# A transformer block on one core: four row blocks of the third unit take their maxima over rectified differences, four later ones no longer do, GpSimd normalises rows in one instruction, and the order of the work is searched anew

## The chip, the cores and the metric

The kernel runs on one core of a Trainium2 chip. A core has TensorE (PE, matrix products into the eight banks of PSUM), VectorE (DVE), ScalarE (ACT), GpSimd (POOL, which works on SBUF alone) and SyncE (SP), which here issues every DMA. The metric is the device time of one execution in microseconds (us), as the median of several runs.

## The reference

A sequence of 2048 rows of 512 is normalised once. The result goes through an attention with 32 heads of 16 and, beside it, through a gated feed-forward layer of width 1792; both are added to the input.

```python
x = A_x                                   # [1, 2048, 512], bf16
xn = _layernorm(x, axis=-1)
# attention: H = 32, Dh = 16
scores = jnp.einsum("bhqd,bhkd->bhqk", q, k) * (Dh ** -0.5)
p = _softmax(scores, axis=-1)
o = jnp.einsum("bhqk,bhkd->bhqd", p, v)
# feed-forward
h = _silu(gate) * up
return x + _A_ref(xn, A_wqkv, A_wo) + _B_ref(xn, B_w1, B_w3, B_w2)
```

## The kernel before, in words

**Tiling.** Four heads make a head group, and 512 queries a query chunk: 8 x 4 pairs of them, the outer loop over chunks. A pair is cut into units of 256 queries (4 x 128 for the last four pairs, 128 + 128 + 256 for the first), 73 units in all. Units 0, 1 and 2 are the first pair.

**Two passes for each unit.** The first pass finds the maximum of each query's scores. TensorE multiplies 128 queries of one head with 512 keys into a PSUM bank (`p1_cand`, L1476), and VectorE reduces two banks at a time to two maxima (L1529, output `part`). One such bank is called a block here; a row block is the four blocks that belong to 128 queries of one head, two reductions. When a unit is complete, `final_max` combines the maxima: on GpSimd for most units (L1651 to L1665), by a small reduction on VectorE (L1688, `negm`) for units 0 and 1 and for those from 62 on. The negative maximum is written beside the queries as two more rows (`Z`, then `QT`), by a matrix product and a copy for units 0, 1 and the last nine (copy on ScalarE L1135, or on VectorE L1131 for the very last), through DMAs for the others. The second pass (`p2_cand`, L1796, or through a block-diagonal copy `BD` of the queries, L835) computes the scores again, keys by queries, now with the maximum subtracted, and ScalarE takes the exponentials into `PT`: one bank (L1821) or, where two lie ready, two banks in one instruction (L1852). `tile_PV` multiplies with the values, whose seventeenth column of ones gives the sums. The last four units are normalised on VectorE (transposes and reciprocal, L1901 to L1905), the others through GpSimd and DMAs.

**Split blocks.** For every second unit from 20 to 42, one row block goes another way: TensorE writes the difference of the scores of two key quarters into a bank (`d_cand`, L1585 and L1588, with the negated queries `QN` made by GpSimd in `split_prep`, L1552), ScalarE rectifies it (L1597, `RB`), and VectorE adds the second quarter and takes the maximum over both pairs in one instruction (L1522, a custom operation with an accumulator). It takes the place of two reductions, and costs ScalarE two Relus.

**The head.** Rows are loaded, their mean and variance taken by VectorE (L872, L875) or ScalarE (L862, L866), the factor by GpSimd (L886, L889). Groups of two row tiles are normalised by VectorE (L902) for the first three groups, and by GpSimd for the other five, as x * r + b: two small operations make b = −mean * r (L893, L895), one applies it (L912). TensorE transposes the result, and products with the weights follow. Keys and queries of the other head groups go through a scratch tensor in DRAM to be spread over partitions: `kq` by ScalarE (L1023), a DMA to `kd` or `qd` (L994), a DMA back into `KT` (L1011) or `QT` (L1016). `HEAD_K` is the position at which the first of these key tiles is due.

**What sets the order.** While the program is built, a planner keeps a time for each engine and picks, again and again, the candidate that can start first among those of the five engines (`pick_dve`, `pick_act`, `pick_pe`, `pick_pool`, `pick_sp`). Rules such as `A_LEAD` (how far ahead of VectorE the first pass is issued) or `PAIR_WAIT` (how long an exponential waits for a second one) may change every twelve positions: `TUNE` names for each stretch an entry of `SETS`. The planner's picks are the program's order on each engine, and each instruction waits on semaphores for what it needs.

## Time and profile before

| | |
|---|---|
| median of 3 runs | 1180.97 us (1180.08 to 1181.68) |
| span of the profiled execution | 1178.6 us (the page gives the span alone for this execution) |
| instructions | 35702 |
| GpSimd busy | 449.4 us (38%) |
| TensorE's granted clock | 1.00 in every stretch of 30 us up to 1170, 0.89 after it |
| chain that ended last | ACT 55%, DVE 31%, PE 11% |

The rest of the profile is shown with the prediction. In its rows, a timeline gives the start, the duration from the first start to the last end, engine, line, operation, output and input with sizes, and how many instructions are merged; in brackets stands the idle time ahead of it and what ended it. Instructions of one engine overlap a little, so the spacing of starts is what one more of them costs. Group rows give count, busy time and mean duration, then the idle time ahead. SPq is SyncE's queue of DMA issues.

### The profile page before, as it was taken

How to read it: one execution, taken by the hardware profiler on the slowest of the kernel's cores; microseconds unless marked ns; L12 is line 12 of the kernel's file. 1: busy time of each engine (PE TensorE's matmuls, PEld its weight loads, DVE VectorE, ACT ScalarE, POOL GpSimd, SP SyncE). 2: the span in 40 equal slices, each digit the busy share in tenths (PEclk: the TensorE clock that was granted, in tenths of full speed). 3: DMA queues.
4: the chain of work that ended last, by engine and by line, in shares of the span. 5: the costliest groups of instructions: out<-in, count | busy, mean ns of one | idle time of the engine just before them, and what ended most of it. 6: DMA issues, size and time to landing. Idle time of an engine off the chain costs nothing.

```text
span 1178.6 us, 35702 instructions
## 1 busy us (share of the span) xinstructions
PE 1111.9 (94%) x14770; PEld 512.0 (43%) x14922; DVE 1165.0 (99%) x1089; ACT 1158.5 (98%) x2130; POOL 449.4 (38%) x886
## 2 busy tenths in 40 slices
PE   8999999999999999999989999999999999899988
PEld 4444334434344433334434444434444443356654
DVE  8999999999999999999999999999999999999996
ACT  8899999999999999999999999999999999999998
POOL 7245534244424246244432222455632126432211
PEclk9999999999999999999999999999999999999999
DMA  8323232111121121111110111221210121001001
GB/s 250 82 70 80 61 91 58 48 29 40 31 49 32 31 67 35 46 39 30 45 27 24 30 43 28 60 52 44 54 30 22 43 57 36 25 22 29 11 11 28
DMA packets 140966, 55.79 MB, mean 47 GB/s; under 512 B 103296, under 2 KB 140804, under 8 KB 140804
## 3 DMA queue, kind: packets, MB, share of 16 engines
q1 hardware_dynamic: 140804, 53.50, 17.7%
q8 instruction: 118, 1.93, 0.7%
q14 instruction: 44, 0.36, 0.1%
HBM read 38.93 MB, written 6.74 MB: 39 GB/s over the span
## 4 chain that ended last, share of the span: by engine, by line
ACT 55%; DVE 31%; PE 11%; issue 1%; DMA 0%; POOL 0%; ACTq 0%; SPq 0%
ACT PT L1821 35%; DVE part L1529 31%; ACT PT L1852 13%; PE ps L835 4%; PE ps L839 3%; PE ps L1796 3%; PE ps L1476 2%; ACT zg L1191 1%; ACT ub L1195 1%; ACT th L1185 1%; ACT RB L1597 1%; ACT U L1919 1%; ACT kq L1023 0%; DMA PT<-in_A_x_dram 0%; ACT osb L1264 0%
## 5 line engine op out<-in xcount | busy, mean ns | idle before, releaser
L1529 DVE TENSOR_REDUCE part<-ps 128x2 f32<-128x1024 f32 x1000 | 1133.9, 1207 | 0.4 <-PE ps L1796 0.2
L1821 ACT ACTIVATE PT<-ps 128x512 bf16<-128x512 f32 x1498 | 799.6, 660 | 2.6 <-PE ps L1796 2.0
L1796 PE MATMUL ps<-QT,KT 32*128 32x256 bf16 (+1 forms) x3768 | 455.1, 258 | 9.0 <-ACT PT L1852 2.8
L1476 PE MATMUL ps<-KT,QT 32*128 32x512 bf16 x2048 | 417.1, 383 | 5.6 <-DVE part L1529 2.1
L1852 ACT ACTIVATE PT<-ps 128x1024 bf16<-128x1024 f32 x275 | 292.2, 1097 | 0.2
L1796 PEld LDWEIGHTS ps<-QT,KT 32*128 32x128 bf16 x3768 | 167.2, 92 | 164.0 <-issue 71.5
L839 PE MATMUL ps<-PT,Vaug 128*17 128x256 bf16 (+1 forms) x4672 | 185.5, 261 | 5.0 <-ACT PT L1852 2.7
L835 PE MATMUL ps<-xnT,ident 128*128 128x512 bf16 (+3 forms) x569 | 151.9, 324 | 24.5 <-ACT PT L1852 7.3
L1476 PEld LDWEIGHTS ps<-KT,QT 32*128 32x128 bf16 x2048 | 104.4, 91 | 141.8 <-issue 59.4
L835 PE MATMUL ps<-xnT,w 128*128 128x512 bf16 (+3 forms) x542 | 141.5, 330 | 8.3 <-ACT U L1919 2.3
L1944 POOL TENSOR_TENSOR Rc<-Lc,mone 128x8 f32<-128x8 f32 (+1 forms) x69 | 104.8, 1519 | 91.6 <-DMA Lc<-U 91.6
L839 PEld LDWEIGHTS ps<-PT,Vaug 128*17 128x17 bf16 x4672 | 88.0, 89 | 75.6 <-issue 51.1
L835 PE MATMUL ps<-BD,KT 128*128 128x256 bf16 (+1 forms) x604 | 103.6, 262 | 0.9 <-ACT PT L1852 0.3
L1658 POOL TENSOR_TENSOR mx<-part 128x16 f32<-128x16 f32 (+1 forms) x60 | 14.2, 236 | 233.9 <-DVE part L1529 233.7
L835 PEld LDWEIGHTS ps<-xnT,ident 128*128 128x128 bf16 x626 | 49.2, 97 | 105.2 <-ACT PT L1821 37.6
L835 PE MATMUL ps<-w,hT 128*128 128x128 bf16 (+3 forms) x326 | 77.9, 304 | 2.3 <-issue 1.0
L1162 POOL TENSOR_SCALAR t<-th 128x512 f32<-128x512 bf16 x56 | 34.7, 620 | 100.8 <-ACT th L1185 99.2
L835 PEld LDWEIGHTS ps<-xnT,w 128*128 128x128 bf16 x584 | 43.1, 97 | 67.4 <-issue 33.3
L1166 POOL TENSOR_TENSOR hT<-a,t 128x512 bf16<-128x512 f32 x56 | 71.0, 1268 | 2.5
L1164 POOL TENSOR_TENSOR a<-zg,ub 128x512 f32<-128x512 bf16 x56 | 64.5, 1153 | 7.5 <-ACT ub L1195 7.5
L835 PEld LDWEIGHTS ps<-BD,KT 128*128 128x128 bf16 x604 | 50.6, 98 | 22.5 <-ACT PT L1852 2.2
L1980 POOL TENSOR_TENSOR on_b<-U,R 128x256 bf16<-128x256 f32 (+1 forms) x33 | 23.4, 710 | 93.6 <-DMA R<-rd 93.5
(114 smaller groups left out, 722.8 us busy)
## 6 DMA issues: line engine op xcount, KB each, us to landing
w<-in_B_w_dram SPq DMA_DIRECT2D x112, 128.0 KB
R<-rd SPq DMA_DIRECT2D x55, 128.0 KB
QT<-qd SPq DMA_DIRECT2D x31, 128.0 KB
KT<-kd SPq DMA_DIRECT2D x28, 128.0 KB
BD<-QT SPq DMA_DIRECT2D x220, 10.5 KB
xr<-in_A_x_dram SPq DMA_DIRECT2D x16, 128.0 KB
out_dram<-osb SPq DMA_DIRECT2D x16, 128.0 KB
qd<-kq SPq DMA_DIRECT2D x15, 128.0 KB
```

Of the source, the lines that this page charges most:

```text
L835: return e.matmul(bank(bk)[:, c0 + a:c0 + b], make_lhsT(0, 128), rhs_ap(0)[:, a:b], start=start, stop=stop, **kw)
L839: ins = e.matmul(bank(bk)[32 * i:32 * i + m, c0 + a:c0 + b], make_lhsT(i), rhs if (a, b) == (0, ncols) else rhs[:, a:b], start=start, stop ...
L1162: q.append(_Item(lambda e: e.tensor_scalar(t1[:, :], th[:, ss, :], 1.0, 1.0, ALU.mult, ALU.add), [("th", ss)], [("t1",)], 0.62, 0.72))
L1164: q.append(_Item(lambda e: e.tensor_tensor(a32[:, :], zg[:, ss, :], ub[:, ss, :], ALU.mult), [("zg", ss), ("ub", ss)], [("a32",)], 1.1, 1.25))
L1166: q.append(_Item(lambda e: e.tensor_tensor(hT[:, hslot(idx), :], a32[:, :], t1[:, :], ALU.mult), [("a32",), ("t1",)], [("hT", hslot(idx))] ...
L1476: ins = e.matmul(bank(held[i]), QT[32 * j:32 * j + 32, qs, q * 128:(q + 1) * 128], KT[32 * j:32 * j + 32, g, c_ * 512:(c_ + 1) * 512], sta ...
L1529: redq.append(_Item(lambda e: e.tensor_reduce(dst, banks, AX.X, ALU.max), writes, [("part", par, i_) for i_ in ix[:m]], _c_dve(512 * m), c ...
L1796: ins = e.matmul(bank(b)[:, i * nq:(i + 1) * nq], KT[32 * j:32 * j + 32, g, (k0 + i) * 128:(k0 + i + 1) * 128], QT[32 * j:32 * j + 32, qs, ...
L1821: expq.append(_Item(lambda e: e.activation(PT[:, sl, :], bank(b), ACTF.Exp, scale=SCALE), [("ps", b)], [("PT", sl)], _c_act(512), cb=cb, e ...
L1852: return _Item(lambda e: e.activation(PT[:, s0:s1 + 1:s1 - s0, :], two_banks(b0, b1), ACTF.Exp, scale=SCALE), [("ps", b0), ("ps", b1)], [( ...
L1944: poolq["nrm"].append(_Item(lambda e: e.tensor_tensor(Rc[:, pp, 0:nl], Lc[:, pp, 0:nl], mone[:, 0:nl], ALU.pow), [("Lc", pp), ("mone",)], ...
L1980: poolq["nrm"].append(_Item(lambda e: e.tensor_tensor(onorm[ob][:, oslot(ob, g), q0:q0 + nq], U[:, us, 0:nq], R[:, pp, 0:nq], ALU.mult), [ ...
```

## The change

Unit 2's first 128 queries have four row blocks, one for each head; all four become split blocks, at the end of the unit's list. Three of them write their rectified differences not to `RB` but to slots 10 to 21 of `hT`, the buffer of the feed-forward layer's inner values, so each of the four has a buffer of its own (`HEAD_LOOK` is the number of positions by which their differences may run ahead). Units 36, 38, 40 and 42 lose their split block. GpSimd's normalisation becomes (x − mean) * r, with the mean as the scalar operand, and the two small operations are gone. `HEAD_K` goes from 14 to 8. The planner's cost of a split block's reduction is raised, and `SETS` and `TUNE` are other tables, with 219 entries instead of 189.

```diff
-    HEAD_K = 14
+    HEAD_K = 8
...
-    SPLITS = ((20, 44, 2), (58, 58, 2))
+    SPLITS = ((20, 36, 2), (58, 58, 2))
+    SPLIT_ROWS = 1
+    HEAD_SPLITS = {2: ((0, 0), (0, 1), (0, 2), (0, 3))}
+    HEAD_BUFS = (10, 14, 18)
+    HEAD_LOOK = 24
...
     SETS = (
         dict(),
-        dict(P2_FRAG=0.0, URG_WAIT=0.05, A_LEAD=0.82, PAIR_WAIT=0.15),
+        dict(FILL_SLIP=0.0, P1_SLIP=0.15),
...
-    SPLIT = {u: ((units[u][3] // 128 - 1, 3),) for lo, hi, st in SPLITS for u in range(lo, hi, st)}
+    SPLIT = {u: tuple((units[u][3] // 128 - 1, 3 - r) for r in range(SPLIT_ROWS)) for lo, hi, st in SPLITS for u in range(lo, hi, st)}
+    SPLIT.update(HEAD_SPLITS)
...
+            rbufs = [(RB[:, :, :], [("RB", 0), ("RB", 1)], [[("RB", 0)], [("RB", 1)]])]
+            for s_ in HEAD_BUFS:
+                rbufs.append((hT[:, s_:s_ + 4, :].rearrange("p a b -> p (a b)").bitcast(FP32)
...
-                               0.5 + 0.16 * (t1 - t0), cb=norm if NORM[gi] == "d" else None))
-                if NORM[gi] != "d":
+                               0.5 + 0.16 * (t1 - t0), cb=None if NORM[gi] == "a" else norm))
+                if NORM[gi] == "a":
...
-                            xn_sb[:, xs, :], x_sb[:, t, :], lnr[:, t:t + 1], lnb[:, t:t + 1], ALU.mult, ALU.add),
-                            [("PT", t), ("lnr", gi), ("lnb", gi)], [("osb", xs)], 0.7, 0.8,
+                            xn_sb[:, xs, :], x_sb[:, t, :], mv[:, t, 0:1], lnr[:, t:t + 1], ALU.subtract, ALU.mult),
+                            [("PT", t), ("lnr", gi), ("mv", t)], [("osb", xs)], 0.7, 0.8,
...
+                if u in HEAD_SPLITS:
+                    ops.append(("S", u, qt, 0, j))
+                    continue
...
-                        out=RB[:, :, :], in0=banks, in1=RB[:, :, :], scale=1.0, scalar=-BIG,
+                        out=rb, in0=banks, in1=rb, scale=1.0, scalar=-BIG,
...
-                        _c_dve(1024) + 0.06, cb=fired, pred=lambda: split_done[n][0] == 2))
+                        writes + rk, rk + [("part", par, ix[0])],
+                        _c_dve(1024) + 0.088, cb=fired, pred=lambda: split_done[n][0] == 2))
...
-                expq.append(_Item(lambda e: e.activation(RB[:, h, :], bank(b), ACTF.Relu),
-                                  [("ps", b)], [("RB", h)], _c_act(512), cb=cb, exp=(b, h, None)))
+                expq.append(_Item(lambda e: e.activation(rb[:, h, :], bank(b), ACTF.Relu),
+                                  [("ps", b)], rh[h], _c_act(512), cb=cb, exp=(b, h, None, bf)))
```

Three places show what the program's order was and is. Lines of the changed kernel stand some 50 further down: its L1582 is L1529 before, L1575 is L1522, L1745 is L1688, L1654 is L1597, L1878 is L1821, L1910 is L1852, L1177 is L1135.

VectorE at the head, from the first reduction through units 0 to 2 and on; before:

```order
L1529 TENSOR_REDUCE part<-ps 128x2
L875 BN_AGGR U<-U 128x2
L1529 TENSOR_REDUCE part<-ps 128x2 x17
L1688 TENSOR_REDUCE negm<-part 128x4
L1529 TENSOR_REDUCE part<-ps 128x2 x2
L1688 TENSOR_REDUCE negm<-part 128x4
L1529 TENSOR_REDUCE part<-ps 128x2 x291
```

and now, where the rows on `hT` and the accumulator reads behind them appear three times and are shown once:

```order
L1582 TENSOR_REDUCE part<-ps 128x2
L917 BN_AGGR U<-U 128x2
L1582 TENSOR_REDUCE part<-ps 128x2 x15
L1745 TENSOR_REDUCE negm<-part 128x4
L1582 TENSOR_REDUCE part<-ps 128x2 x3
L1745 TENSOR_REDUCE negm<-part 128x4
L1582 TENSOR_REDUCE part<-ps 128x2 x5
L1575 ISA RB,part<-ps,RB 128x1024
L1575 ISA part 128x1
L1575 ISA hT,part<-ps,hT 128x1024
```

The maximum of unit 0 stands behind 16 reductions instead of 18, and units 0 to 2 take 24 reductions and four split blocks instead of 32 reductions.

ScalarE around the first query copy (`QT`, which follows unit 0's maximum); `Vaug` are the values, `kq` the keys and queries of other head groups; before:

```order
L968 ACTIVATE KT<-ps,kbias 128x512
L1023 ACTIVATE kq<-ps 128x512
L1038 ACTIVATE Vaug<-ps 128x32x16 x2
L1135 ACTIVATE QT<-ps 128x128
L1038 ACTIVATE Vaug<-ps 128x32x16
L1852 ACTIVATE PT<-ps 128x1024
```

and now:

```order
L1010 ACTIVATE KT<-ps,kbias 128x512
L1065 ACTIVATE kq<-ps 128x512
L1654 ACTIVATE RB<-ps 128x512
L1080 ACTIVATE Vaug<-ps 128x32x16
L1654 ACTIVATE RB<-ps 128x512
L1654 ACTIVATE hT<-ps 128x512
L1177 ACTIVATE QT<-ps 128x128
L1080 ACTIVATE Vaug<-ps 128x32x16
L1654 ACTIVATE hT<-ps 128x512
L1878 ACTIVATE PT<-ps 128x512
```

Three Relus stand ahead of the first query copy and five behind it; the last of the eight is the twenty-first instruction of 512 columns behind that copy, with one more query copy between.

The tail: VectorE from the maximum of the last unit but one, before:

```order
L1688 TENSOR_REDUCE negm<-part 128x4
L1529 TENSOR_REDUCE part<-ps 128x2 x6
L1901 STREAM_TRANSPOSE RB<-ps 128x128
L1902 RECIPROCAL RB<-RB 128x4
L1903 STREAM_TRANSPOSE R<-RB 128x128
L1905 TENSOR_TENSOR wk_on<-ps,R 128x128
L1529 TENSOR_REDUCE part<-ps 128x2
```

and now:

```order
L1745 TENSOR_REDUCE negm<-part 128x4
L1582 TENSOR_REDUCE part<-ps 128x2 x7
L1745 TENSOR_REDUCE negm<-part 128x4
L1690 TENSOR_SCALAR Z<-negm 128x4
L1692 TENSOR_TENSOR Z<-negm,Z 128x4
L1959 STREAM_TRANSPOSE RB<-ps 128x128
```

The normalisation of unit 69 moved from ahead of the last reduction to behind the last maximum. On ScalarE, behind the last query copy there (L1135 before, L1177 now), stood 17 single and 11 double exponentials, and there are 19 single and 8 double ones now. Over the whole program single ones go from 1498 to 1538 and double ones from 275 to 255; reductions of two banks go from 1000 to 998, beside one of three banks and one of a single bank, and split blocks stay at 12.

In SyncE's queue the second key write (`kd`) moved from behind the loads of `wo` and `wol` to ahead of them, right behind the first key fetch; the third and fourth stand behind eight copies to `BD`, those of units 0 and 1.

## The prediction

> **What bounds the kernel now.** I read the busy times of the engines, then the table of 30 us stretches, then VectorE's (DVE) and ScalarE's (ACT) timelines at the head and the tail.

> ```profile
> PE 1111.9 (94%) x14770; PEld 512.0 (43%) x14922; DVE 1165.0 (99%) x1089; ACT 1158.5 (98%) x2130; POOL 449.4 (38%) x886
> 0.00:30.00 30.00, 26.80 (x203) 14.75 (x206) 26.58 (x44) 24.20 (x55) 21.18 (x51) 1.00 0.79 246
> 30.00:60.00 30.00, 29.20 (x284) 13.35 (x291) 29.93 (x29) 25.44 (x49) 5.54 (x14) 1.00 0.32 85
> 60.00:90.00 30.00, 29.36 (x429) 13.64 (x426) 30.00 (x27) 29.19 (x54) 14.76 (x27) 1.00 0.27 64
> ...
> 570.00:600.00 30.00, 27.80 (x342) 11.85 (x334) 30.00 (x28) 30.00 (x53) 13.42 (x25) 1.00 0.15 36
> ```

> The columns after the length are PE, PEld, DVE, ACT and POOL busy, then clock and DMA. VectorE has no idle time after the head; ScalarE's idle time also lies in the first 90 us: 5.80 + 4.56 + 0.81 = 11.2 us. The shares of 99% and 98% do not say which of the two ends last. VectorE's timeline does.

> ```profile
> 13.79 1.23 DVE L1529 TENSOR_REDUCE part<-ps 128x2 f32<-128x1024 f32 x1
> 14.93 0.17 DVE L875 BATCH_NORM_AGGREGATE U<-U 128x2 f32<-128x6 f32 x1
> 15.02 19.29 DVE L1529 TENSOR_REDUCE part<-ps 128x2 f32<-128x1024 f32 x17
> 34.34 0.18 DVE L1688 TENSOR_REDUCE negm<-part 128x4 f32<-128x16 f32 x1
> ...
> 366.10 1.21 DVE L1522 CUSTOM_DVE_ANT_0 RB<-ps,RB 128x1024 f32<-128x1024 f32 x1
> 367.24 0.08 DVE L1522 DVE_READ_ACCUMULATOR2_ANT part<- 128x1 f32 x1
> 367.24 34.02 DVE L1529 TENSOR_REDUCE part<-ps 128x2 f32<-128x1024 f32 x30
> 401.18 1.20 DVE L1522 CUSTOM_DVE_ANT_0 RB<-ps,RB 128x1024 f32<-128x1024 f32 x1
> ```

> Thirty reductions take 401.18 − 367.24 = 33.94 us, 1.131 us each. A rectified block (L1522) takes 1.14 us to the next start, at most 1.22 with its accumulator read. Now the tail.

> ```profile
> 1152.98 0.17 DVE L1688 TENSOR_REDUCE negm<-part 128x4 f32<-128x16 f32 x1
> 1153.07 6.87 DVE L1529 TENSOR_REDUCE part<-ps 128x2 f32<-128x1024 f32 x6
> 1159.86 0.30 DVE L1901 STREAM_TRANSPOSE RB<-ps 128x128 f32<-128x128 f32 x1
> ...
> 1160.97 1.21 DVE L1529 TENSOR_REDUCE part<-ps 128x2 f32<-128x1024 f32 x1
> 1162.21 0.18 DVE L1688 TENSOR_REDUCE negm<-part 128x4 f32<-128x16 f32 x1
> ...
> 1164.11 0.28 DVE L1131 TENSOR_SCALAR QT<-ps 128x128 bf16<-128x128 f32 x1
> ```

> From 15.02 to the last maximum at 1162.21 are 1147.2 us. The work in it is 999 reductions x 1.131 = 1129.9, 12 rectified blocks x 1.14 to 1.22 = 13.7 to 14.6, 12 unit maxima x 0.09 = 1.1 and one normalisation of 1160.97 − 1159.86 = 1.1: 1145.8 to 1146.7. At most 1.4 us of 1147 are waits. **VectorE's work is the bound** up to 1162; after that comes the last unit's chain (query copy at 1164.11, sixteen exp blocks, product, output). ScalarE runs close behind:

> ```profile
> 1154.52 0.30 ACT L1135 ACTIVATE QT<-ps 128x128 bf16<-128x128 f32 x1
> 1154.68 6.55 ACT L1821 ACTIVATE PT<-ps 128x512 bf16<-128x512 f32 x13
> 1161.11 2.86 ACT L1852 ACTIVATE PT<-ps 128x1024 bf16<-128x1024 f32 x3
> 1163.82 0.64 ACT L1821 ACTIVATE PT<-ps 128x512 bf16<-128x512 f32 x1
> 1164.30 2.00 ACT L1852 ACTIVATE PT<-ps 128x1024 bf16<-128x1024 f32 x2
> ...
> 1169.35 3.92 ACT L1852 ACTIVATE PT<-ps 128x1024 bf16<-128x1024 f32 x4
> ```

> A single exp costs (1161.11 − 1154.68)/13 = 0.49 us, a pair (1163.82 − 1161.11)/3 = 0.90. From 1164.30 to 1173.27 ScalarE works 8.97 us where the last unit alone, as eight pairs, needs 7.2: it is 1.7 us in arrears. So relieving ScalarE can win 1.7 us and no more, unless VectorE ends earlier too.

> **The change, part by part.** *Split blocks.* Unit 2 swaps eight reductions for four rectified blocks: VectorE 4 x (2.26 − 1.14 to 1.22) = 4.2 to 4.5 us less in the head. ScalarE gets 8 Relus. Units 36 to 42 get the same amounts back with opposite sign. The changed program has 12 rectified blocks as before, and 998 double, one triple and one single reduction for 1000 double ones. Triple and single have no row; together they read as many elements in as many instructions, so I take 0, with 0.6 us (half a reduction) either way as bounds. **VectorE's total is unchanged**, and since it has no idle time, its last maximum can't move by this.

> *Relus in the head.* Their group has the price, and the stretch in which they land has the room:

> ```profile
> L1597 ACT ACTIVATE RB<-ps 128x512 f32<-128x512 f32 x24 | 15.3, 646 | 0.1
> 25.00:36.00 11.00, 10.95 (x71) 4.31 (x70) 10.96 (x12) 6.26 (x12) 8.21 (x9) 1.00 0.59 183
> 35.63 0.28 ACT L1135 ACTIVATE QT<-ps 128x128 bf16<-128x128 f32 x1 [0.65 <-PE ps L835]
> ```

> At a single's spacing (0.646 us long, as an exp) eight cost 3.9 us, beside 4.7 us of idle time between 25 and 36 us: hidden there, and the later 3.9 us are free for exps. The new wait is VectorE's, and every later reduction stands behind it. The fourth rectified block is due at 15.02 + 23 x 1.131 + 0.2 + 3 x 1.22 = 44.9. The last Relu: unit 0's maximum comes after 16 reductions, at 32.1; its query copy followed 35.63 − 34.34 = 1.3 later, so 33.4; from there the new order has 21 ScalarE instructions of 0.49 and two short ones, 10.6 us, end with latency 44.1. That is 0.8 us early if ScalarE never waits. If the 4.7 us of idle time came back behind TensorE, VectorE would stop 4.0 us. Bounds 0 and 4.0; the row with continuous work (36 us on) is nearer, I take 0.2.

> *GpSimd.* Ten small operations go:

> ```profile
> L893 POOL TENSOR_TENSOR U<-U 128x2 f32<-128x2 f32 x5 | 1.0, 196 | 0.2
> L895 POOL TENSOR_SCALAR U<-U 128x2 f32<-128x2 f32 x5 | 1.0, 192 | 0.5
> ```

> 0.39 us for each of five groups, 1.9 in all, on the way to the later key quarters. VectorE does not wait for those (no idle after 13.79), so 0; the cover can't be lost, the chain only gets shorter. The normalisation itself keeps its form, two per-row scalars. Four part copies (0.2 each) now stand ahead of unit 2's maximum, which starts 4 us earlier; 0.

> *Keys and scratch.* Unit 3 starts at 41.2 + 4 x 1.22 = 46.1 instead of 15.02 + 31 x 1.131 + 0.2 = 50.3 and needs its keys as much earlier. Before, SP's queue (SPq) did this for the second key quarter, behind the loads of wo:

> ```profile
> 37.34 0.59 SPq L994 DMA_DIRECT2D kd<-kq  x1
> 38.03 3.11 SPq L1615 DMA_DIRECT2D BD<-QT  x4
> 41.24 0.86 SPq L1011 DMA_DIRECT2D KT<-kd  x2
> ...
> 58.66 0.59 ACT L1191 ACTIVATE zg<-ps 128x512 bf16<-128x512 f32 x1
> ```

> The new order puts that write ahead of the wo loads. The third quarter's stands behind eight BD copies, of which the last four start with unit 1's query copy (unit 1's maximum at 32.1 + 3 x 1.131 + 0.1 = 35.6, then 1.3 as for unit 0, and a microsecond of queue: about 38): written at 41, fetched 3.9 later as above, with 2 us (an estimate) for landing there at 47, against a need at 46.1 + 2 x 4.5 = 55.1. The fourth follows unit 2's maximum: about 54 against 59.7. Cost 0; another set of BD copies ahead, 3.1 us, would still pass. The scratch slots of hT are written by the feed-forward part only, whose first gate leaves ScalarE at 58.66, after 46.1.

> *New order, tail.* VectorE's normalisation of unit 69 (1.1 us) stood ahead of the last reduction; it now stands behind the last maximum, beside ScalarE's exps. The last maximum comes at 1161.1, the last query copy at 1163.0. On ScalarE, the copy that follows 1152.98 is now followed by 19 singles and 8 pairs, 16.5 us, where 17 and 11 took 18.3: **1.7 us less**, four blocks fewer in arrears. Both chains shift alike, so the exps end near 1171.5 and not 1173.27. Overall ScalarE gets 20 pairs fewer and 40 singles more, +1.6 us, paid from its idle time in the head.

> *Last matmuls.*

> ```profile
> 1167.47 0.81 PE L835 MATMUL ps<-wol,wk_on 128*128 128x512 bf16 x3 [0.16 <-issue]
> 1173.95 1.70 PE L835 MATMUL ps<-wol,wk_on 128*128 128x512 bf16 x3 [0.23 <-issue]
> 1170.00:1174.00 4.00, 1.82 (x73) 1.28 (x70) 0.55 (x2) 3.27 (x4) 0.45 (x1) 0.97 0.26 86
> 1174.00:1178.60 4.60, 1.62 (x3) 0.21 (x2) 1.57 (x5) 0.00 (x0) 0.00 (x0) 0.50 0.08 29
> ```

> Three equal matmuls take 0.81 us at clock 1.00 and 1.70 at 0.50, after four microseconds with TensorE 1.82 busy. Where the clock drops decides 0.9 us. I leave them slow, since the new tail has the same gaps; bounds −0.9 and 0. [...]

> **Sum.** The profiled execution's span is 1178.6; the median of the runs is 1180.97, 2.4 more, which I take as constant. 1180.97 − 1.7 (tail) + 0.2 (head) = **1179.5**; with the triple and what waits may remain, 1178.6 to 1180.2. A measurement of this kernel can tell about 0.2% (2.4 us) from no change.

> **The rivals.** (a) *The shift does not carry*: ScalarE waits for TensorE at the head, VectorE for the late Relus, and the tail's 1.7 us are spent before they are seen. For: ScalarE waited on TensorE all through 25 to 36 us. Against: the 0.8 us in hand. With a stop of 1 to 3 us it gives 1180.3 to 1182.3, mid 1181. This is also the case in which the change does nothing.

> (b) *More than the tail*: the clock drop is missed (−0.9) and of the 1.4 us of waits half go: 1178.0. For: the runs before differ by 1.6 us. Against: two lucky things at once.

> (c) *The new order feeds VectorE worse*, slower. Every stretch is ordered anew, and TensorE fills PSUM banks just ahead of each reduction.

> ```profile
> L1821 ACT ACTIVATE PT<-ps 128x512 bf16<-128x512 f32 x1498 | 799.6, 660 | 2.6 <-PE ps L1796 2.0
> L1919 ACT ACTIVATE U<-ps 128x256 f32<-128x256 f32 (+1 forms) x69 | 29.1, 422 | 2.5 <-PE ps L839 2.5
> ```

> ScalarE already waits 5.1 us in these two groups, nearly all for TensorE. If VectorE came to wait as much for its banks, nothing could make it up: 1179.3 + 5.1 = 1184.4. It decides from 4 ns per reduction on. Against: at most 1.4 us before, in an order made by the same planner.

> **How the numbers follow.** Forecast 0.50; (a) 0.22; (b) 0.18; (c) 0.10. The range 1177.7 to 1182.4 leaves out half of (c) and the outer edges of (a) and (b). Faster by over 0.2% (under 1178.6): (b) and a sliver of the forecast, 0.20. Slower (over 1183.3): most of (c) and an edge of (a), 0.10. Within: 0.70.

> **What would show it.** Right: VectorE's last maximum near 1161, the four rectified blocks in a row near 41 to 46 with no idle time before them, ScalarE idle in the first 90 us down from 11.2 to about 8, last exp ending near 1171.5. Wrong: idle time of VectorE before a rectified block, or released by TensorE in the middle; or a last maximum at 1162 or later.

## The result, and the profile after

The changed kernel takes 1196.58 us in the median of four runs (1196.17 to 1197.02), the kernel before 1181.33 beside it: a ratio of 1.0118 (95% interval 1.0087 to 1.0149). The four runs of the kernel before lie between 1180.08 and 1189.23, and the ratios here are worked out over all runs, so they are not quite the quotients of the medians. The changed kernel is 15 us slower. The forecast was 1179.5, its range ended at 1182.4, and slower by over 0.2% had a chance of 0.10.

The profiled execution took 1196.17 us, 2.2 more than its span. First the page of the changed kernel: its span, its busy times and the granted clock in 40 slices.

```profile
span 1194.0 us, 35666 instructions
...
PE 1114.0 (93%) x14757; PEld 512.8 (43%) x14899; DVE 1166.5 (98%) x1089; ACT 1160.7 (97%) x2150; POOL 461.5 (39%) x873
...
PEclk9799999999999999999999999999999999999999
```

VectorE has 1.5 us more work than before (1166.5 against 1165.0), and ScalarE 2.2. The 15 us are therefore waits. POOL is GpSimd; it is 12.1 us busier, although it has 13 instructions fewer (873 for 886; none of them, before or now, reads or writes a PSUM bank). The table of 30 us stretches says when it happened (columns as before).

```profile
0.00:30.00 30.00, 21.75 (x154) 12.40 (x156) 20.47 (x38) 20.00 (x46) 22.34 (x34) 0.91 0.77 239
30.00:60.00 30.00, 26.31 (x172) 9.95 (x176) 21.04 (x23) 17.89 (x36) 14.66 (x16) 0.74 0.22 60
60.00:90.00 30.00, 28.81 (x402) 13.80 (x404) 29.94 (x29) 29.28 (x59) 5.31 (x20) 1.00 0.20 51
```

In the first 60 us VectorE works 41.51 us where it worked 56.51 before: 15.0 us are lost there and hardly any after. TensorE (PE) is idle more as well, and its clock, 1.00 in these stretches before, is 0.91 and 0.74. The waits of the changed kernel, in the views of VectorE, of TensorE and of ScalarE, give the chain (total, times, longest).

```profile
DVE part L1582 <- PE ps L1528: 15.9, 12, 2.9
```

```profile
PE ps L979 <- POOL osb L954: 8.8, 8, 1.9
```

```profile
ACT xnT L986 <- PE ps L979: 9.8, 7, 2.0
```

VectorE's reductions (L1582) wait for the score products (L1528). The transposes that TensorE does on the way to them (L979) wait for GpSimd's normalisation (L954), and ScalarE's copies of these (L986) wait for the transposes. The group row of that normalisation among GpSimd's groups, first of the changed kernel, then of the kernel before:

```profile
L954 POOL TENSOR_SCALAR osb<-PT,U 128x512 bf16<-128x512 bf16 x10 | 20.7, 2075 | 0.4
```

```profile
L912 POOL TENSOR_SCALAR osb<-PT,U 128x512 bf16<-128x512 bf16 x10 | 7.7, 770 | 0.7
```

It is the same instruction on the same tiles with the same number of scalars, and takes 2.075 us instead of 0.770. Ten of them make 10 x 1.305 = 13.05 us more. GpSimd's timeline begins the first two at 12.26 and ends the last two at 37.62, with 0.4 us of idle time ahead of all ten (the group row's last figure):

```profile
12.26 4.15 POOL L954 TENSOR_SCALAR osb<-PT,U 128x512 bf16<-128x512 bf16 x2
...
33.49 4.13 POOL L954 TENSOR_SCALAR osb<-PT,U 128x512 bf16<-128x512 bf16 x2
```

VectorE's timeline of the changed kernel shows the same stretch from its side; in brackets stands the idle time ahead and what ended it:

```profile
26.74 1.22 DVE L1582 TENSOR_REDUCE part<-ps 128x2 f32<-128x1024 f32 x1 [2.88 <-PE ps L1528]
...
47.93 0.18 DVE L1745 TENSOR_REDUCE negm<-part 128x4 f32<-128x16 f32 x1
...
57.34 1.21 DVE L1575 CUSTOM_DVE_ANT_0 RB<-ps,RB 128x1024 f32<-128x1024 f32 x1
```

Unit 0's maximum starts at 47.93, where it started at 34.34 before, although it now stands behind two reductions fewer.

The tail of the changed kernel: from VectorE's timeline the maximum of the last unit but one, from ScalarE's the last exp.

```profile
1170.29 0.17 DVE L1745 TENSOR_REDUCE negm<-part 128x4 f32<-128x16 f32 x1
```

```profile
1188.07 0.80 ACT L1878 ACTIVATE PT<-ps 128x512 bf16<-128x512 f32 x1
```

From the one to the end of the other are 1188.87 − 1170.29 = 18.6 us; before, 1173.27 − 1152.98 = 20.3. The tail's gain of 1.7 us is there, as forecast.

### The profile page after: what moved, and what is told of

Same layout as the page of the kernel before. It is cut to its first block, busy times and chain, and to the rows that moved or that the text cites. A ratio compares the mean times of both kernels' runs of the same rounds, so it can differ in the third digit from the quotient of the medians.

```text
span 1194.0 us, 35666 instructions
## 1 busy us (share of the span) xinstructions
PE 1114.0 (93%) x14757; PEld 512.8 (43%) x14899; DVE 1166.5 (98%) x1089; ACT 1160.7 (97%) x2150; POOL 461.5 (39%) x873
## 4 chain that ended last, share of the span: by engine, by line
ACT 70%; PE 15%; DVE 11%; POOL 3%; issue 1%; ACTq 0%; POOLq 0%
ACT PT L1878 46%; ACT PT L1910 15%; DVE part L1582 11%; PE ps L877 6%; PE ps L1853 3%; PE ps L881 3%; PE ps L1528 2%; ACT zg L1233 2%; ACT ub L1237 2%; ACT th L1227 2%; POOL osb L954 2%; ACT U L1977 1%; ACT kq L1065 1%; ACT RB L1654 1%; PE ps L2239 1%
## 5 line engine op out<-in xcount | busy, mean ns | idle before, releaser
L1582 DVE TENSOR_REDUCE part<-ps 128x2 f32<-128x1024 f32 x1000 | 1135.0, 1216 | 16.0 <-PE ps L1528 15.9
L1878 ACT ACTIVATE PT<-ps 128x512 bf16<-128x512 f32 x1538 | 822.3, 672 | 2.8 <-PE ps L877 1.0
L1528 PE MATMUL ps<-KT,QT 32*128 32x512 bf16 x2036 | 417.0, 385 | 5.5 <-DVE part L1582 3.1
L1910 ACT ACTIVATE PT<-ps 128x1024 bf16<-128x1024 f32 x255 | 275.3, 1114 | 0.0
L881 PE MATMUL ps<-PT,Vaug 128*17 128x256 bf16 (+1 forms) x4672 | 189.7, 261 | 4.5 <-DVE part L1582 1.5
L1528 PEld LDWEIGHTS ps<-KT,QT 32*128 32x128 bf16 x2036 | 103.6, 91 | 145.1 <-issue 72.7
L1715 POOL TENSOR_TENSOR mx<-part 128x16 f32<-128x16 f32 (+1 forms) x60 | 14.2, 236 | 223.1 <-DVE part L1582 222.9
L877 PE MATMUL ps<-BD,KT 128*128 128x256 bf16 (+1 forms) x574 | 98.5, 262 | 1.5 <-ACT PT L1910 0.9
L877 PE MATMUL ps<-w,hT 128*128 128x512 bf16 (+3 forms) x322 | 75.5, 307 | 3.4 <-ACT U L1977 1.9
L877 PEld LDWEIGHTS ps<-xnT,w 128*128 128x128 bf16 x610 | 45.9, 97 | 70.4 <-issue 36.1
L881 PE MATMUL ps<-BD,KT 128*32 128x256 bf16 (+1 forms) x1272 | 58.4, 265 | 0.2
L877 PEld LDWEIGHTS ps<-BD,KT 128*128 128x128 bf16 x574 | 48.1, 98 | 22.3 <-ACT PT L1910 1.9
```

Of the source, the lines that this page charges most:

```text
L877: return e.matmul(bank(bk)[:, c0 + a:c0 + b], make_lhsT(0, 128), rhs_ap(0)[:, a:b], start=start, stop=stop, **kw)
L881: ins = e.matmul(bank(bk)[32 * i:32 * i + m, c0 + a:c0 + b], make_lhsT(i), rhs if (a, b) == (0, ncols) else rhs[:, a:b], start=start, stop ...
L1528: ins = e.matmul(bank(held[i]), QT[32 * j:32 * j + 32, qs, q * 128:(q + 1) * 128], KT[32 * j:32 * j + 32, g, c_ * 512:(c_ + 1) * 512], sta ...
L1582: redq.append(_Item(lambda e: e.tensor_reduce(dst, banks, AX.X, ALU.max), writes, [("part", par, i_) for i_ in ix[:m]], _c_dve(512 * m), c ...
L1878: expq.append(_Item(lambda e: e.activation(PT[:, sl, :], bank(b), ACTF.Exp, scale=SCALE), [("ps", b)], [("PT", sl)], _c_act(512), cb=cb, e ...
L1910: return _Item(lambda e: e.activation(PT[:, s0:s1 + 1:s1 - s0, :], two_banks(b0, b1), ACTF.Exp, scale=SCALE), [("ps", b0), ("ps", b1)], [( ...
```

## The experiments

The first theory (A in the texts) is that the pair of operations makes the instruction slow: (subtract, mult) now, (mult, add) before. Its rivals are the other things that changed with it, the operands' source and the order of the work. Except in the fourth and the eighth experiment the order on VectorE, ScalarE, TensorE and SyncE is that of the kernel in which the edit is made, repeated instructions apart.

**1. The old pair of operations in the changed kernel.**

```diff
-  xn_sb[:, xs, :], x_sb[:, t, :], mv[:, t, 0:1], lnr[:, t:t + 1], ALU.subtract, ALU.mult),
+  xn_sb[:, xs, :], x_sb[:, t, :], mv[:, t, 0:1], lnr[:, t:t + 1], ALU.mult, ALU.add),
```

> The changed kernel with one edit: GpSimd's ten normalisations use the operations (mult, add) in place of (subtract, mult), with the same operands, so that they compute x * mean + r, not the normalised rows; the order on every engine stays as it is. Theory A, the pair of operations is what is slow on GpSimd: each of the ten takes about 0.77 us and not 2.07, VectorE's 16 us of waits fall to under 2, TensorE's clock stays at 1.00 from 20 to 50 us, and the time is what the sum gave, 1179.5 us (1178 to 1181). Rival B, the operands (the mean as a scalar, taken from the statistics) are slow: still 2.07 us each, about 1196.6. Rival C, the four rectified blocks and the new order starve VectorE by themselves: 0.77 us each, but most of the waits stay, over 1188.

Measured: 1180.76 us (12 runs), ratio 0.9992 (0.9978 to 1.0006). The group of the normalisation and VectorE's wait in this run:

```profile
L954 POOL TENSOR_SCALAR osb<-PT,U 128x512 bf16<-128x512 bf16 x10 | 7.6, 769 | 0.4
```

```profile
DVE part L1582 <- PE ps L1528: 1.1, 3, 0.6
```

With nothing else altered the instruction is back at 0.769 us, VectorE's wait falls from 15.9 to 1.1, and the whole 15.8 us (1196.58 − 1180.76) are gone. The time lies in theory A's 1178 to 1181, near its upper end. The pair of operations is the cause of the 15 us; the operands, the rectified blocks and the new order are not.

**2. Ten pairs, one for each tile.**

```diff
+  PAIRS = ((ALU.mult, ALU.add), (ALU.add, ALU.mult), (ALU.subtract, ALU.mult), (ALU.mult, ALU.subtract),
+           (ALU.mult, ALU.mult), (ALU.add, ALU.add), (ALU.subtract, ALU.add), (ALU.max, ALU.mult),
+           (ALU.subtract, ALU.subtract), (ALU.mult, ALU.max))
...
-  xn_sb[:, xs, :], x_sb[:, t, :], mv[:, t, 0:1], lnr[:, t:t + 1], ALU.subtract, ALU.mult),
+  xn_sb[:, xs, :], x_sb[:, t, :], mv[:, t, 0:1], lnr[:, t:t + 1], *PAIRS[t - 6]),
```

> The changed kernel with a different pair of operations in each of the ten normalisations of GpSimd (row tiles 6 to 15: mult add, add mult, subtract mult, mult subtract, mult mult, add add, subtract add, max mult, subtract subtract, mult max); the rows are not normalised by most of them. Read for the duration of each alone. Theory A1, only mult followed by add has a fast form: 0.77 us for tile 6 and about 2.07 for the nine others. A2, a leading subtract is slow: 2.07 for tiles 8, 12 and 14, 0.77 for the rest. A3, any subtract is slow: tiles 8, 9, 12 and 14 slow. Under A2, mult followed by subtract would be a correct and quick way to normalise. Under rival B all ten take 2.07.

Measured: 1190.69 us in one run. GpSimd's timeline of this run, in the order of the list (four lines more in the source shift the number to L958; a row holds as many tiles as its last figure says):

```profile
12.17 1.53 POOL L958 TENSOR_SCALAR osb<-PT,U 128x512 bf16<-128x512 bf16 x2
...
15.55 2.08 POOL L958 TENSOR_SCALAR osb<-PT,U 128x512 bf16<-128x512 bf16 x1
...
18.33 2.08 POOL L958 TENSOR_SCALAR osb<-PT,U 128x512 bf16<-128x512 bf16 x1
...
20.78 0.77 POOL L958 TENSOR_SCALAR osb<-PT,U 128x512 bf16<-128x512 bf16 x1
...
22.24 6.24 POOL L958 TENSOR_SCALAR osb<-PT,U 128x512 bf16<-128x512 bf16 x3
...
29.65 4.15 POOL L958 TENSOR_SCALAR osb<-PT,U 128x512 bf16<-128x512 bf16 x2
```

(mult, add) and (add, mult) take 1.53 together, (mult, mult) 0.77; the other seven take 2.08 each (6.24 for three in a row, 4.15 for two), (add, add) and (mult, max) among them. Each pair stands in one tile only here. None of the three versions of theory A in the expectation fits in full: it is neither the subtraction alone nor its place. The ten pairs show two durations, 0.77 and 2.08 us, and no run shows what makes a pair quick. Of use here is (add, mult).

**3. The new pair in the kernel before.**

```diff
-  xn_sb[:, xs, :], x_sb[:, t, :], lnr[:, t:t + 1], lnb[:, t:t + 1], ALU.mult, ALU.add),
+  xn_sb[:, xs, :], x_sb[:, t, :], lnr[:, t:t + 1], lnb[:, t:t + 1], ALU.subtract, ALU.mult),
```

> The kernel before with one edit: its ten normalisations use (subtract, mult) in place of (mult, add), with the same operands, so that they compute (x - r) * b; order unchanged, no rectified blocks in the head. Theory A: 2.07 us each, ten times 1.31 us more on GpSimd's chain, VectorE waits 10 to 17 us in the first 60 us, 1192 to 1199 us. Rival B (operands): 0.77 us each and about 1181. Rival C (the new order and the head blocks are to blame): 2.07 us each, but hidden, under 1184.

Measured: 1193.07 us (four runs), ratio 1.0099 (1.0083 to 1.0114): 11.8 us over the kernel before in these runs (1181.28), with 11.7 us of new wait ahead of VectorE's reductions:

```profile
DVE part L1529 <- PE ps L1476: 11.7, 10, 2.5
```

Each normalisation takes 2.08 us in this run too. TensorE's clock is at half for 10.24 us as well, from 25.88, so the 11.8 us hold that loss too (experiments 6, 7 and 9). So the new pair of operations, put into the kernel before by itself, costs most of what the whole change cost.

**4. The old normalisation, small operations and all, in the changed kernel.** The planner places its instructions anew for it, with tables that were searched for other costs.

```diff
-  0.5 + 0.16 * (t1 - t0), cb=None if NORM[gi] == "a" else norm))
-  if NORM[gi] == "a":
+  0.5 + 0.16 * (t1 - t0), cb=norm if NORM[gi] == "d" else None))
+  if NORM[gi] != "d":
...
-  xn_sb[:, xs, :], x_sb[:, t, :], mv[:, t, 0:1], lnr[:, t:t + 1], ALU.subtract, ALU.mult),
+  xn_sb[:, xs, :], x_sb[:, t, :], lnr[:, t:t + 1], lnb[:, t:t + 1], ALU.mult, ALU.add),
```

> The changed kernel with the normalisation of before put back (two small operations, then mult and add), result as the reference's; the planner makes its order anew under the changed tables, which were searched for other costs. Theory A: no long waits in the head, 1179.5 plus what an order that was not searched for costs, which I take as 0 to 6 us: 1179 to 1186. Rival C: the head blocks still starve VectorE, over 1188.

Measured: 1208.29 us (four runs), ratio 1.0226 (1.0206 to 1.0247). A miss by more than 20 us, and one that the head does not explain. The windows of this run and, below them, of the kernel before:

```profile
0.00:60.00 60.00, 55.18 (x456) 27.68 (x463) 54.39 (x73) 49.35 (x104) 27.82 (x69) 1.00 0.53 163
60.00:1140.00 1080.00, 1023.29 (x13151) 470.02 (x13279) 1078.48 (x969) 1065.76 (x2032) 413.20 (x796) 1.00 0.17 42
1140.00:1206.00 66.00, 51.89 (x1221) 30.82 (x1230) 34.51 (x50) 58.12 (x93) 10.03 (x19) 0.97 0.07 17
```

```profile
0.00:60.00 60.00, 56.00 (x485) 28.10 (x497) 56.51 (x72) 49.64 (x104) 26.73 (x64) 1.00 0.55 165
60.00:1140.00 1080.00, 1023.94 (x13552) 464.93 (x13682) 1079.69 (x974) 1075.55 (x1970) 417.22 (x811) 1.00 0.17 42
1140.00:1178.60 38.60, 31.95 (x751) 18.93 (x752) 28.77 (x45) 33.27 (x59) 5.43 (x11) 0.94 0.09 23
```

ScalarE is idle for 14.2 us between 60 and 1140, where it was for 4.5, and has 58.12 + 1065.76 + 49.35 = 1173.2 us of work instead of 1158.5, since fewer exponentials found a partner (177 pairs, where the changed kernel has 255). With 9.8 us more idle time and 14.8 more work it arrives at the end some 25 us in arrears, and VectorE, done early, waits for it. That looks like the price of an order that was not searched for its costs; experiment 8 tests whether such an order can cost that much. The profiled run, 1205.12, was the shortest of the four; the others had a lower mean granted clock (0.997 to 0.992 for 0.999), so some of the 27 us in the median are the clock's.

**5. A pair that computes the normalisation and is quick: (x + (−mean)) * r.**

```diff
-  q = poolq["ln"]
+  q, neg = poolq["ln"], lambda e: e.tensor_scalar(lnb[:, sl_], mv[:, sl_, 0], -1.0, 0.0, ALU.mult, ALU.add)
...
-  q.append(_Item(lambda e: e.tensor_tensor(lnr[:, sl_], lnt[:, sl_], mhalf[:, sl_], ALU.pow),
+  q.append(_Item(lambda e: [neg(e), e.tensor_tensor(lnr[:, sl_], lnt[:, sl_], mhalf[:, sl_], ALU.pow)][1],
...
-  xn_sb[:, xs, :], x_sb[:, t, :], mv[:, t, 0:1], lnr[:, t:t + 1], ALU.subtract, ALU.mult),
+  xn_sb[:, xs, :], x_sb[:, t, :], lnb[:, t:t + 1], lnr[:, t:t + 1], ALU.add, ALU.mult),
```

> The changed kernel with a normalisation that computes the same thing by another pair of operations: (x + (-mean)) * r, as add and mult, with -mean made by one small GpSimd instruction (128x2, 0.19 us) ahead of the power of each of the eight groups. The order on the other four engines is the same. Theory A (the pair of operations is the whole loss): ten normalisations of 0.77 us, VectorE's waits at the reductions of two banks about 1 us, and a time like that of the first experiment (1180.8) plus at most 5 x 0.28 = 1.4 us for the small instructions on GpSimd's chain, so 1180.3 to 1182.5, and no difference from the kernel before that can be measured. Rival (what is left of the change is worth the 1.5 us that the prediction forecast once the pair is right): 1179.0 to 1179.8. Rival (one rounded scalar less, a mean as scalar operand costs by itself): 2.07 us each and about 1196.

Measured: 1181.04 us (12 runs), ratio 0.9979 (0.9957 to 1.0001). The group of the normalisation in this run, then VectorE's timeline at the head and at the tail:

```profile
L954 POOL TENSOR_SCALAR osb<-PT,U 128x512 bf16<-128x512 bf16 x10 | 7.7, 772 | 0.4
```

```profile
13.76 1.19 DVE L1582 TENSOR_REDUCE part<-ps 128x2 f32<-128x1024 f32 x1
...
41.84 1.21 DVE L1575 CUSTOM_DVE_ANT_0 RB<-ps,RB 128x1024 f32<-128x1024 f32 x1
...
44.41 1.23 DVE L1575 CUSTOM_DVE_ANT_0 hT<-ps,hT 128x1024 f32<-128x1024 f32 x1 [0.20 <-PE ps L1645]
```

```profile
1154.54 0.17 DVE L1745 TENSOR_REDUCE negm<-part 128x4 f32<-128x16 f32 x1
...
1162.66 0.18 DVE L1745 TENSOR_REDUCE negm<-part 128x4 f32<-128x16 f32 x1
```

Theory A again: this is the rest of the change with a quick normalisation, and it cannot be told from the kernel before. The median lies in theory A's bounds and above those of the rival that gave it the full 1.5 us of the forecast (at most 1179.8), though the interval alone would allow both. The traces, one of each kernel, speak for A: VectorE starts where it started before (13.76 against 13.79), but reaches the maximum of the last unit but one 1154.54 − 1152.98 = 1.6 us later, which takes back nearly all of the tail's gain. Some gain may be left: the median span is 1178.95 us against 1179.9 for the kernel before.

**6. The slow pair for the last four of the ten tiles only.**

```diff
-  ALU.subtract, ALU.mult),
+  *((ALU.mult, ALU.add) if t < 12 else (ALU.subtract, ALU.mult))),
```

> The changed kernel with (mult, add) for the first six of the ten tiles on GpSimd, and (subtract, mult) for the last four, order and operands unchanged; the first six tiles become x * mean + r instead of the normalised rows. If GpSimd's chain is serial and without slack from the first tile on, the loss over the all-fast version (1180.8) is 4 x 1.31 = 5.2 us, and the time 1186.0. If the chain has slack (the reductions of the head run without a wait from 15.5 to 32.7 us in the all-fast version), a part of it is hidden: 1182 to 1185. If the loss is mostly TensorE's half clock, which set in at about 25 us, behind the longest wait for GpSimd: more than 5.2 where the clock falls here too (1186.5 to 1188), and the granted clock between 25 and 45 us shows whether it did.

Measured: 1187.38 us (ten runs), ratio 1.0041 (1.0023 to 1.0060): 6.6 us over the first experiment, where four times 1.31 are 5.2. That is the third case of the expectation. The windows of the profiled run:

```profile
30.00:35.00 5.00, 4.33 (x15) 1.42 (x17) 1.71 (x2) 1.20 (x2) 5.00 (x5) 0.52 0.35 94
35.00:40.00 5.00, 4.78 (x16) 1.11 (x16) 3.19 (x3) 1.29 (x2) 1.59 (x1) 0.50 0.43 124
```

TensorE is busy for 4.33 and 4.78 of 5 us there and the clock, the last but two of the columns, is 0.52 and 0.50: behind the wait for GpSimd stands a second candidate for the loss, TensorE at half speed. This run was the longest of the ten (1189.65). The mean granted clock of the ten lies between 0.995 and 0.999, which over some 1185 us is 5.9 to 1.2 us of clock lost, and single runs don't follow it: the one at 0.999 took 1187.35, the one at 0.995 took 1187.28. So this trace alone does not show what the half clock costs.

**7. The slow pair throughout, and a TensorE that is kept busy while it waits.**

```diff
-  for c in range(DC):
+  for c in list(range(DC)) * (6 if 7 <= t < 15 else 1):
       ins = e.transpose(tb[:, c, :], xn_sb[:, xs, c * 128:(c + 1) * 128], ident[:, :])
```

> The changed kernel, slow pair and all, with TensorE's transposes of eight of the ten tiles (the second to the ninth that GpSimd normalises) written six times over, with the same result: 20 more matmuls of 128 columns a tile, about 1.1 us at full clock, in time in which TensorE waits for GpSimd. If a TensorE that is too little busy is what halved its clock between 25 and 45 us, the clock stays near 1.00 there, the score products behind GpSimd's last tile (10.3 us from the end of the normalisation to the first unit's maximum, 7.9 in the all-fast version) run faster, and the time falls by 1 to 2.5 us: 1194.0 to 1195.5. If the half clock is without weight (everything there waits for GpSimd anyway), the time is 1196 to 1197. If the clock falls in spite of it, the repeated transposes take 2.2 us a tile, longer than GpSimd's 2.07, and the time rises: 1197 to 1200.

Measured: 1191.89 us (seven runs, 1191.6 to 1192.34), ratio 1.0077 (1.0048 to 1.0105). Windows of this run, then of the changed kernel itself:

```profile
25.00:35.00 10.00, 9.84 (x146) 8.20 (x145) 4.05 (x5) 4.56 (x9) 9.73 (x8) 1.00 0.79 256
35.00:45.00 10.00, 9.89 (x72) 4.10 (x72) 8.80 (x9) 5.88 (x11) 8.71 (x8) 1.00 0.33 86
```

```profile
25.00:35.00 10.00, 6.35 (x28) 2.27 (x28) 3.67 (x3) 3.37 (x6) 9.73 (x8) 0.50 0.69 232
35.00:45.00 10.00, 8.49 (x30) 2.38 (x30) 4.90 (x4) 3.17 (x5) 8.69 (x6) 0.50 0.27 74
```

160 more matmuls, and the kernel is 4.7 us faster (1196.58 − 1191.89), with GpSimd as slow as ever (9.73 of 10 us busy in both). The direction was expected, the size not: I gave the clock 1 to 2.5 us. At half clock the products take longer: in the changed kernel one of 128x512 took 0.63 us at 42.44, at a clock of 0.50, and 0.39 at 1190.65, at 1.00. What is left, 1191.89 − 1180.76 = 11.1 us, I put down to GpSimd, whose last normalisation ends 12.6 us later here than in the first experiment (37.43 against 24.86).

**8. The kernel before, with one constant of the planner changed and all its work the same.**

```diff
-  _c_dve(1024) + 0.06, cb=fired, pred=lambda: split_done[n][0] == 2))
+  _c_dve(1024) + 0.088, cb=fired, pred=lambda: split_done[n][0] == 2))
```

> The kernel before with one planner's constant changed (the cost of a split block's reduction, 0.06 to 0.088, as in the change), and its own tables, which were not searched for that constant; the work is the same, the order is another. If an order that wasn't searched for its costs is what made the fourth experiment (the changed kernel with the old normalisation) 27 us slow: 1190 to 1215, with the loss spread over the program or at its end, not at the head. If the old normalisation itself was the cause there: 1180 to 1184.

Measured: 1196.86 us (two runs), ratio 1.0116 (1.0060 to 1.0171). 0.028 us in a cost that the planner only reads, and the kernel is 15 us slower. The two runs took 1198.60 us at a mean clock of 0.995, which is the profiled one, and 1195.12 at 1.000, so the order costs some 13.5 us with hardly any clock lost. The windows:

```profile
60.00:1140.00 1080.00, 1033.36 (x13317) 472.15 (x13437) 1076.34 (x969) 1068.46 (x2038) 414.81 (x805) 1.00 0.17 42
1140.00:1197.00 57.00, 50.44 (x1129) 29.23 (x1134) 34.82 (x51) 50.89 (x91) 8.54 (x17) 0.98 0.07 18
```

The pattern is that of the fourth experiment: ScalarE idle for 11.5 us in the long middle, then a tail of 57 us. So an unsearched order alone can cost about half of what the fourth experiment lost, and that experiment says nothing of the normalisation. That its whole 27 us come from the order and the clock is likely by its rows and was not shown.

**9. Four slow tiles, as in the sixth, with TensorE kept busy as in the seventh.**

```diff
-  for c in range(DC):
+  for c in list(range(DC)) * (6 if 11 <= t < 15 else 1):
```

> The sixth experiment (four slow tiles; the first six tiles become x * mean + r) with the transposes of the sixth to the ninth tile that GpSimd normalises written six times over, as in the seventh. If the loss is GpSimd's delay less a slack, plus the half clock: the seventh run has 12.6 us of delay on GpSimd and 11.1 us at the end, so a slack of 1.5; four tiles delay by 5.2, which leaves 3.7 over 1180.8, and a time of 1184.5 (1183.8 to 1185.2) with the granted clock at 1.00 from 20 to 45 us, where the sixth had 0.50 for ten of them and 1187.4. If four slow tiles cost 6.6 us by their own, the repeated transposes change nothing or add: 1187 to 1189.

Measured: 1184.35 us (12 runs, 1183.73 to 1184.63), ratio 1.0021 (1.0013 to 1.0030), inside the expected 1183.8 to 1185.2. Two of the windows:

```profile
30.00:35.00 5.00, 5.00 (x35) 1.91 (x33) 3.87 (x5) 2.37 (x4) 5.00 (x5) 1.00 0.34 96
35.00:40.00 5.00, 5.00 (x40) 1.93 (x39) 4.96 (x7) 3.67 (x8) 1.85 (x3) 1.00 0.51 141
```

The clock stays at 1.00 (0.999 or 1.000 in the mean of each of the 12 runs) and 3.0 of the 6.6 us go. This experiment ran on another chip than the first eight, where the kernel before took 1181.63 us, against 1181.28 and 1181.66. The two pairs of runs side by side (in us, losses over the 1180.76 of the first experiment):

| slow tiles | more work on GpSimd | loss left with TensorE kept busy | loss that this takes away | whole loss |
|---|---|---|---|---|
| 4 | 4 x 1.31 = 5.2 | 3.6 | 3.0 | 6.6 |
| 10 | 10 x 1.31 = 13.1 | 11.1 | 4.7 | 15.8 |

The fourth column goes with the clock: the repeated transposes hold it at 1.00 from 20 to 45 us, and the order and GpSimd's times stay what they were. That the clock alone is worth it is argued, since single runs of the sixth experiment do not follow their clocks.

Between 5.2 and 3.6, and between 13.1 and 11.1, lie 1.6 and 2.0 us that the head had in hand. By the end of the last normalisation, 5.5 and 12.6 us later than in the first experiment, it is 1.9 and 1.4. The fifth experiment shows a part of this room: its last normalisation ends 0.6 us later than in the first (25.48 against 24.86), and the maximum of unit 0 is not later for it (32.47 against 32.73).

## Why the prediction was wrong

**The step that failed** is GpSimd's part of the change: "The normalisation itself keeps its form, two per-row scalars", and with it "the cover can't be lost, the chain only gets shorter". The form was kept and the two operations in it were not, and the duration hangs on these: 0.77 us became 2.07, ten times over. The quoted cost of nothing should have had a row, and it had none: the trace of before shows L912 as TENSOR_SCALAR and does not show its operations, so (subtract, mult) was an operation that no row showed and was to be bounded from both sides. The dearest arithmetic row of 128x512 on GpSimd before was at 1.27 us (L1166); as an upper bound it would have put ten times half a microsecond on the slower side. That is still less than the ten times 1.3 that were measured.

**The cover.** "VectorE does not wait for those, so 0" took the lack of a wait for room without end. The room was some 1.5 to 2 us (experiments 7 and 9), and a chain that is 13 us longer goes through it: VectorE's reductions waited 15.9 us.

**The clock** was weighed at the tail alone, for 0.9 us. At the head, keeping TensorE busy and its clock at 1.00 was worth 4.7 us. From 1170 to the end of the span the kernel before had a granted clock of 0.72 (the 0.89 of the table is that of a stretch to 1200, beyond the span). At the tail the prediction left the last products slow, and the changed kernel's last one took 0.39 us, full clock; yet from the end of the last exp to the end of the span went 5.1 us for 5.3, so at most 0.2 of the 0.9 was won.

**The tail was right.** 1.7 us were forecast from the numbers of singles and pairs behind the query copy of the last unit but one, and 18.6 us for 20.3 are measured; the same in the fifth experiment (1173.13 − 1154.54).

**The head was nearly right, once the normalisation is quick.** In the fifth experiment the four rectified blocks stand in a row from 41.84 to 46.85, with one wait of 0.20 where 0.2 was forecast. That the numbers agree is luck: the forecast had the fourth block wait for a late Relu, and here the third waits for TensorE. ScalarE's idle time in the first 90 us is 8.2 us (by its windows 6.04 + 2.06 + 0.10) where about 8 was.

**VectorE's total was off by a little.** That "its last maximum can't move by this" failed: it should have come near 1161, since one normalisation stood behind it, and came at 1162.66 even in the fifth experiment. Summed from start to start in the two traces, the 993 reductions ahead of the maximum at 1154.54 take 1125.6 us for 1124.5 (0.6 of the difference is idle time ahead of one, 0.5 are longer steps), and the twelve rectified blocks with their accumulator reads 14.1 for 13.7, the wait of 0.20 among them. That is the 1.6 us. The triple and the single reduction take 2.26 us, as two double ones do, so the 0 that was taken for them was right. The outcome is that of rival (a), "the tail's 1.7 us are spent before they are seen", though not by the late Relus that it named, and the fifth experiment's 1181.0 is the time that it was given. Which piece of the new order spends them stays open: an order with one piece taken back would have to be searched for its own costs (experiment 8), and was not tried.

**The 2 us for a landing** that the prediction took for a key fetch are an estimate; the nearest wait in the kernel before is that of SyncE's queue for the writes of `kd` to land, 6.0 us in three times and at most 2.4:

```profile
SPq L1011 <- DMA kd<-kq: 6.0, 3, 2.4
```

**The 2.4 us outside the span** were no constant. Each run on record has its own span: the kernel before takes 1.7 us outside it in the median, and the order of the changed kernel 2.1, in the first and fifth experiment as in the changed kernel itself. So 0.4 us of what the new order may gain in the span is lost outside it. With 1.7 outside it the span of 1178.6 belongs to a time of some 1180.3, below the median of 1180.97.

**The rivals.** (c), a slower kernel, named the new order and TensorE's banks. The slower kernel came, and VectorE did wait for TensorE, but for a reason that stood in none of the cases.

## What to carry to other kernels

An instruction's price can belong to its operations as well as to its kind and shape, here 0.77 or 2.08 us: where a change swaps the operations, take the new one for unpriced until a row shows it. A wait that a profile does not show is room of unknown size, so measure how early the chain is before calling its cover safe. Before an experiment lets a planner place the work anew, run one that alters nothing but the placing.

## What the runs showed of the hardware

**The half clock lasted 20.48, 10.24 and 3.42 us in three traces.** Rows of one microsecond of the changed kernel, the sixth and the seventh experiment, in that order (the clock is the last column but two):

```profile
24.00:25.00 1.00, 0.00 (x0) 0.00 (x0) 0.00 (x0) 0.15 (x1) 1.00 (x1) 0.92 0.54 151
45.00:46.00 1.00, 1.00 (x6) 0.34 (x6) 0.46 (x1) 0.14 (x1) 0.00 (x0) 0.84 0.25 65
```

```profile
30.00:31.00 1.00, 0.33 (x4) 0.36 (x5) 0.00 (x0) 0.00 (x0) 1.00 (x3) 0.58 0.67 136
40.00:41.00 1.00, 1.00 (x6) 0.22 (x4) 0.47 (x1) 0.24 (x1) 0.00 (x0) 0.80 0.05 12
```

```profile
16.00:17.00 1.00, 0.73 (x9) 0.73 (x10) 0.37 (x1) 0.00 (x0) 0.83 (x3) 0.76 0.63 176
19.00:20.00 1.00, 1.00 (x4) 0.30 (x2) 0.00 (x0) 1.00 (x3) 1.00 (x1) 0.53 0.00 0
```

In between the clock is 0.50. A mean of 0.92 therefore means half clock for the last 0.16 us, so it began at 24.84; 0.84 puts its end at 45.32. The three stretches last 20.48, 10.24 and 3.42 us: six, three and one times 3.41. TensorE's rows of the 3.41 us that end with the fall, in the changed kernel and in the seventh experiment, and of a stretch of the second experiment that did not end so (busy time, then the clock):

```profile
21.43:24.84 3.41, 1.52 (x14) 1.00 0.28 75
```

```profile
13.11:16.52 3.41, 1.82 (x16) 1.00 1.08 261
```

```profile
20.39:23.81 3.42, 1.81 (x15) 1.00 0.46 108
```

TensorE was busy for 45% and 53% of the two stretches that ended with the fall, and for 53% of the one that did not. A trace can lack the record of a product: in the first of these rows two weight loads for products with `hT` start at 23.30, and one such product is shown, at 23.36. One of 128x512 would add 0.2 to 0.4 us (three in a row take 0.81, one alone 0.39), so the shares may be too low by some 6 to 12 points. Either way TensorE was idle for some 1.2 to 1.9 us of the 3.41 ahead of the fall, and busy time alone does not draw the line. What does, no run here shows.
